# One pool of eight PSUM banks, and a biased order of work, in a kernel of two memory-attention and two gated layers

## The chip, the cores and the metric

The kernel runs on one core of one Trainium2 chip. The metric is the device time of one execution in microseconds (us), lower is better. Every time quoted is the median of the runs that are named with it; all runs here were in the same (fast) state, with a mean granted TensorE clock of 0.982 to 0.996 in their records. (The granted clock is the share of full speed at which the chip let TensorE run.) A ratio is the mean time of one kernel's runs over the mean of the other's runs of the same rounds, so it is not quite the ratio of the medians quoted beside it. Engines: PE is TensorE's matmul, PEld its weight load, DVE is VectorE, ACT is ScalarE, POOL is GpSimd.

## The reference, cut to what matters

Two layers of a memory-augmented attention A and a gated feed-forward B, applied twice with the same weights:

```python
x = x + A(layernorm(x));  x = x + B(layernorm(x))      # and the same two lines once more

def A(x):                            # 2048 rows, width 448, 16 heads of 256
    mem = mem0                       # 8 rows
    for s in range(64):              # 64 segments of 32 rows, one after the other
        h = concat([mem, x[32*s : 32*s+32]])             # 40 rows
        q, k, v = h @ Wq, h @ Wk, h @ Wv                 # per head
        p = softmax(mask(q @ k.T / 16))
        o = (p @ v) @ Wo
        mem = o[:8]                  # the next segment needs this
        outs.append(o[8:])

def B(x):                            # relu-gated: 448 -> 1792 -> 448
    return (relu(x @ Wg) * (x @ Wu)) @ Wd
```

The loop over segments is a recurrence: segment s+1 cannot form its keys before the eight memory rows of segment s are known. Layer 2 runs four segments behind layer 1, in the same matmuls, so there are 68 steps. Two steps are a pair; B is done once per pair.

## The kernel before

The kernel folds `Wq` with `Wk` into `M` and `Wv` with `Wo` into `N` once at the start. TensorE writes its results into eight PSUM banks, tensors of 128 x 512 float32; a copy of a result out of a bank by DVE or ACT is called an eviction below. Each step is made of small kinds of work, which the argument below calls by these names:

| kind | what TensorE does in it |
|---|---|
| `t_unit` | T = M times the step's 40 columns `hT`, 224 matmuls of 80 columns; DVE/ACT copy them to `TTm` and `TTs` |
| `s_mem`, `p_t_mem`, `u_mem`, `un_mem` | scores of the memory rows, transpose of P, U = P times `hK`, memory output = `UTm` times `N` (in 32-column tiles) |
| `m_t` | eight small selection matmuls that bring the new memory rows (kept as two bf16 tensors, `hi` and the rest `lo`), transposed, into `hT` (the T units of the next step need them) |
| `m_nat` | two matmuls that bring the same rows in natural layout into `hK` |
| `s_seg`, `seg_pt`, `u_seg` | the same for the 32 segment rows; U goes to `U` (inside the tensor named `big`) |
| `un` | attention output of a pair, 56 matmuls of 448 columns, `U` times `N` |
| `ln_b`, `b_layer`, `b_down`, `ln_a` | layer norm, gate/up, down, and the layer norm that makes the input of a later pair |

The program is first a list of operations with the keys that they read and write. (A tile in the code is a result that occupies a bank. The changes of tiling further below are another thing: TensorE's array, divided into parts for small matmuls.) A list scheduler then orders the operations with a model of the engines, and the engines run in that order. An operation's priority is the length of the longest path behind it:

```python
class _Order:
    POOLS = {"R": [0, 1, 2, 3, 5]}                     # five banks in a pool
    LAT = {"pe": 170.0, "act": 0.0, "dve": 0.0, ...}

    def graph(self):
        ...
        for o in reversed(self.ops):
            lat = ...
            o.prio = min(o.cost.values()) + max([q.prio + ... for q in o.succs], default=lat)

    def run(self):
        ...                     # for each engine: when could each candidate start?
            t0 = min(x[0] for x in lst)
            lim = max(f, t0) + (60.0 if e == "pe" else 40.0)
            t, o = max((x for x in lst if x[0] <= lim), key=lambda x: (x[1].prio, -x[0]))
        ...
        for tl in o.alloc:      # a tile takes the bank of its pool that is free first
            b = min(fr, key=lambda k: fr[k])
```

The other three banks have fixed roles: bank 4 (`bO`) for `un` and `b_down`, banks 6 and 7 (`bC`) for the memory's chain:

```python
self.bO, self.bC = bank[4], bank[6:8]

def m_t(self, t):
    b1, b0 = S.bC[1], S.bC[0]                                          # banks 7 and 6
    S.mm(... three groups into b1 ..., S.ps(7))
    S.mm(... the fourth group into b0[:, 448:464] ..., S.ps(6))
    S.cp(hT[..., 0:3, ...], b1[...], 48, S.ps(7), w, eng=("dve",))
    for half in range(2):
        S.cp(hT[64*half:..., 3, ...], b0[64:128, 448:464], 16, S.ps(6, half=(1,)), ..., eng=("act",))

def m_nat(self, t):
    b0 = S.bC[0]                                                       # bank 6 again
    S.mm(lambda: [MM(b0[:, 0:D], S.seln[:, :], x[:, :], ...) for i, x in enumerate((S.hi, S.lo))], ..., S.ps(6))
```

A last detail: the code that sets the semaphores lets two engines take turns on a bank even when both only read it.

```python
            if r[0] == "ps":
                for src, val in self.readers.get(r, {}).items():
                    if src != eng:
                        want(src, val)
```

Of the kernel before, what the change touches and what calls it, by code (L numbers as in the profile page):

```python
# [6 lines left out]
BF = dt.bfloat16  # L7
# [142 lines left out]

class _Tile:
# [12 lines left out]
class _Op:  # L164
    __slots__ = ("kind", "eng", "cost", "fn", "rd", "wr", "name", "mode", "preds", "succs", "prio", "np", "fin", "alloc", "tiles", "fixed", "lat")


class _Order:
# [5 lines left out]
    POOLS = {"R": [0, 1, 2, 3, 5]}  # L174

    def __init__(self, sched):
        self.sc = sched
        self.ops = []

    def add(self, kind, eng, cost, fn, rd, wr, name=None, mode=0, lat=None):  # L180
        o = _Op()
        o.kind, o.eng, o.cost, o.fn, o.rd, o.wr, o.name, o.mode = kind, eng, cost, fn, list(rd), list(wr), name, mode
        o.succs, o.np, o.alloc, o.fixed, o.lat = [], 0, [], None, lat
        self.ops.append(o)
        return o
# [9 lines left out]
    def graph(self):  # L195
# [26 lines left out]
        for o in reversed(self.ops):  # L222
            lat = self.LAT[o.eng[0]] if o.lat is None else o.lat
            o.prio = min(o.cost.values()) + max([q.prio + (0.0 if o.kind == q.kind == "pe" else lat + 60.0) for q in o.succs], default=lat)

# [143 lines left out]
class _Kernel:  # L369
# [16 lines left out]
    def alloc(self):  # L386
# [46 lines left out]
        self.bO, self.bC = bank[4], bank[6:8]  # L433
# [355 lines left out]
    def s_mem(self, t):  # L789
# [4 lines left out]
        b = S.bC[0]  # L794
        S.mm(lambda: [MM(b[:, l * KEYS:l * KEYS + KEYS], S.TTm[:, c, l, :], S.hT[:, pp, s, c, l, :], start=(c == 3), stop=(c == 2))
                      for l in range(l0, l1) for c in (3, 0, 1, 2)], 100.0 * nl,
             [("TTm",) + k for k in S.TKEYS] + [("hTx", pp, s)] + S.mkeys(pp, s, l0, l1), S.ps(6))
        st = S.stat
        src = b[:, l0 * KEYS:l1 * KEYS].rearrange("p (l x) -> p l x", l=nl)
# [3 lines left out]
        S.dve(lambda E: E.tensor_reduce(st[:, 32:32 + nl], src, AX.X, ALU.max), n, S.ps(6), [("sm", 0)])  # L803
        S.dve(lambda E: E.tensor_tensor(Em, src, bc(32), ALU.subtract), n, S.ps(6) + [("sm", 0)], [("Em",)])
# [51 lines left out]
    def p_t_mem(self, t):  # L856
        S = self
        pT = S.bC[1][:, :].bitcast(BF)
        S.mm(lambda: [MM(pT[:, 0:128], S.Pm[:, :], S.ident[:, :], is_transpose=True)], 60.0, [("Pm",), ("ident",)], S.ps(7))
        S.cp(lambda: S.PTm[:, :], lambda: pT[:, 0:128], 128, S.ps(7), [("PTm",)])  # L860
# [10 lines left out]
    def u_mem(self, t):  # L871
# [3 lines left out]
        S.mm(lambda: [m for c in range(4) for l in range(l0, l1) for m in S.u_mms(l, c, pp, s, S.bC[l][:, c * 128:], S.PTm, 8)], 350.0,  # L875
             [("PTm",)] + [("hKx", pp, s, l) for l in range(l0, l1)] + [("hKm", pp, s, l) for l in range(l0, l1)],
             S.ps(*[6 + l for l in range(l0, l1)]), mode=1)
        for l in range(l0, l1):
            S.cp(lambda l=l: S.UTm[:, 0:NO, l * 8:l * 8 + 8], lambda l=l: S.bC[l][:, 0:D].rearrange("p (o q) -> p o q", o=NO), D,
                 S.ps(6 + l), [("UTm", l)], eng=("act", "dve") if l1 - l0 == 1 else (("act", "dve")[l],))  # L880

    def un_mem(self, t):
        S = self
        b = S.bC[0]

        def mms():
            out = []
            for k in range(14):
                for j in range(4):
                    o = 14 * j + k  # L890
                    lhs = S.UTm[:, o:o + 2, :].rearrange("p a q -> p (a q)")
                    out.append(MM(b[32 * j:32 * j + 32, 0:D], lhs, S.N[:, o, :], start=(k == 0), stop=(k == 13)))
            return out

        S.mm(mms, 14 * S.pitch(D) + 100.0, [("UTm", 0), ("UTm", 1)] + (S.Nkeys if t == 0 else []), S.ps(6), mode=2)
        S.act(lambda E: E.activation(S.hi[:, :], b[:, 0:D], ACT.Copy), D, S.ps(6), [("hi",)])  # L896
        S.dve(lambda E: E.tensor_tensor(S.lo[:, :], b[:, 0:D], S.hi[:, :], ALU.subtract), D, S.ps(6) + [("hi",)], [("lo",)])  # L897

    def m_t(self, t):
# [5 lines left out]
        b1, b0 = S.bC[1], S.bC[0]  # L905
        sel = [("sel", j) for j in range(4)]
        S.mm(lambda: [MM(b1[:, c * 16:c * 16 + 16], x[:, c * 128:c * 128 + 128], S.selm[:, :], start=(i == 0), stop=(i == 1))
                      for c in range(3) for i, x in enumerate((S.hi, S.lo))], 150.0, [("hi",), ("lo",)] + sel, S.ps(7))
        S.mm(lambda: [MM(b0[:, 448:464], x[:, 320:448], S.selm[:, :], start=(i == 0), stop=(i == 1)) for i, x in enumerate((S.hi, S.lo))],
             50.0, [("hi",), ("lo",)] + sel, S.ps(6))  # L910
        w = [("hTm", pp, s, l) for l in range(l0, l1)]
        S.cp(lambda: S.hT[:, pp, s, 0:3, l0:l1, SEG:KEYS], lambda: b1[:, 0:48].rearrange("p (c l q) -> p c l q", c=3, l=2)[:, :, l0:l1, :],
             48, S.ps(7), w, eng=("dve",))
        v = b0[64:128, 448:464].rearrange("p (l q) -> p l q", l=2)[:, l0:l1, :]
        for half in range(2):
            S.cp(lambda half=half: S.hT[64 * half:64 * half + 64, pp, s, 3, l0:l1, SEG:KEYS], lambda: v, 16, S.ps(6, half=(1,)),
                 [("hTm3", pp, s, half)], eng=("act",))

    def m_nat(self, t):
# [3 lines left out]
        b0 = S.bC[0]  # L923
        S.mm(lambda: [MM(b0[:, 0:D], S.seln[:, :], x[:, :], start=(i == 0), stop=(i == 1)) for i, x in enumerate((S.hi, S.lo))],
             2 * S.pitch(D), [("hi",), ("lo",), ("sel",)] + [("sel", j) for j in range(4)], S.ps(6))
        for l in range(*S.layers(t)):
            if l == 1 and t == LAG:
                continue
# [153 lines left out]
```

## Time and profile before

1785.34 us, median of 3 runs (1779.55 to 1785.48). The profile's first part gives each engine's busy time, its share of the span and its instructions:

```profile
span 1780.3 us, 67770 instructions
PE 1700.7 (96%) x30612; PEld 1226.7 (69%) x30612; DVE 1073.2 (60%) x3058; ACT 720.6 (40%) x2031; POOL 91.0 (5%) x156
```

TensorE bounds the kernel, and the other engines have room. But a busy share of 96% does not say how much could be won, because a matmul's record is longer than the distance to the next one. So I worked from the starts of the matmuls in the trace. A matmul of 448 columns starts 189 ns after the one before, one of 128 columns 56 ns, one of 80 columns 36 ns, and one of 40 columns or fewer 25 ns. Where the tiles of the array change (whole array, 40 rows, 32 or 64 columns), the next start comes 95 ns later than that. Whatever remains of the distance between two starts is called waiting here. This splits the time from the first matmul to the last:

| before | us |
|---|---|
| all matmuls at their own pitch | 1578.5 |
| 721 changes of tiling, 95 ns each | 68.5 |
| waiting | 121.9 |
| of it steps 0 to 10 (with the weight loads) / steps 10 to 60 / the end | 37.8 / 65.0 / 19.1 |

Where the waiting is shows the view of who waited for whom. A line reads: engine, line and tile that waited, what it waited for, us in total, times, longest. These are TensorE's waits for copies of `hT`, for `xn` (the layer norm's output) and for the evictions of U (`big`):

```profile
PEld b L127 <- ACT hT L684: 30.1, 80, 0.6
PEld b L127 <- DVE xn L721: 27.4, 31, 5.6
PEld b L127 <- ACT big L684: 21.0, 47, 0.7
PE b L127 <- ACT hT L684: 14.9, 32, 0.5
PEld b L127 <- DVE big L685: 14.5, 28, 0.7
```

The longest regular one, in the timeline (start, duration, engine, line, operation, tiles, shape, count, idle before and releaser):

```profile
823.99 0.17 PE L127 MATMUL b<-selm,lo 128*128 128x16 bf16 x1
824.01 0.62 DVE L968 TENSOR_TENSOR XB<-b,XA 128x448 bf16<-128x448 f32 x1 [0.50 <-PE b L127]
824.20 0.38 ACT L684 ACTIVATE hT<-b 64x16 bf16<-64x16 f32 x2 [0.19 <-PE b L127]
824.55 0.20 DVE L685 CAST hT<-b 128x48 bf16<-128x48 f32 x1
...
824.64 0.36 PE L127 MATMUL b<-hi,seln 128*128 128x448 bf16 x1 [0.48 <-ACT hT L684]
```

The last selection matmul starts at 823.99. The natural-layout matmul (`hi,seln`) could follow at once, but it writes bank 6, which ACT still reads for `hT`, and it starts 0.65 us later.

### The profile page before, as it was taken

Reading aid. Unit: us, or ns where it says so; the run is one execution under the profiler, and the core shown is the slowest. Engines: PE = TensorE matmul, PEld = TensorE weight load, DVE = VectorE, ACT = ScalarE, POOL = GpSimd, SP = SyncE. Lnnn points to the kernel's source line nnn. Section 1 sums busy time; section 2 is a strip of 40 time slices with the busy share of each in tenths; the row PEclk is TensorE's granted clock in tenths of the full one; section 3 lists DMA queues with packets and bytes.
Section 4 is the critical chain, followed back from the end, with each engine's and each line's share of the span. In section 5 each row is a group of like instructions: output and inputs, shape, how many; then the busy total and the mean of one; then the engine's idle time right before and its main releaser. Section 6 shows DMA issues by size and latency. Waiting matters only on the chain.

```text
span 1780.3 us, 67770 instructions
## 1 busy us (share of the span) xinstructions
PE 1700.7 (96%) x30612; PEld 1226.7 (69%) x30612; DVE 1073.2 (60%) x3058; ACT 720.6 (40%) x2031; POOL 91.0 (5%) x156
## 2 busy tenths in 40 slices
PE   6899999999999999999999999999999999999997
PEld 2566766777677667767766776776677677667765
DVE  7647565565656556565655656565665656566554
ACT  5433433444443334444333444334344433434432
POOL 3000000000000000000000000000000000000000
PEclk9999999999999999999999999999999999999999
DMA  9700000000000000000000000000000000000000
GB/s 227 219 4 4 4 5 5 4 5 5 5 4 5 5 4 5 5 5 4 5 5 4 5 5 5 4 5 4 4 5 6 5 4 5 3 3 4 4 4 5
DMA packets 55760, 27.52 MB, mean 15 GB/s; under 512 B 44584, under 2 KB 54576, under 8 KB 55472
## 3 DMA queue, kind: packets, MB, share of 16 engines
q1 hardware_dynamic: 55120, 22.94, 5.3%
q8 instruction: 241, 3.95, 0.9%
q14 instruction: 47, 0.39, 0.1%
q10 hardware_dynamic: 352, 0.24, 0.1%
HBM read 10.33 MB, written 1.84 MB: 7 GB/s over the span
## 4 chain that ended last, share of the span: by engine, by line
PE 75%; DVE 6%; ACT 2%; issue 1%; DVEq 0%
PE b L127 75%; ACT big L684 1%; DVE big L685 1%; DVE stat L714 1%; DVE TTs L685 1%; DVE xn L721 1%; ACT hT L684 1%; DVE ys L1015 1%; DVE XA L1008 1%; DVE XB L968 0%; DVE Es L843 0%; DVE stat L842 0%; DVE TTm L685 0%; DVE hT L685 0%; DVE part L957 0%
## 5 line engine op out<-in xcount | busy, mean ns | idle before, releaser
L127 PEld LDWEIGHTS b<-hT,Mw 128*128 128x128 bf16 x15232 | 539.8, 100 | 25.3 <-DVE hT L685 11.2
L127 PE MATMUL b<-hT,Mw 128*128 128x80 bf16 (+1 forms) x15232 | 546.0, 200 | 5.0 <-DVE hT L685 4.6
L127 PE MATMUL b<-Nw,big 128*128 128x448 bf16 (+1 forms) x1936 | 394.9, 358 | 8.2 <-DVE big L685 5.6
L685 DVE CAST TTs<-b 128x320 bf16<-128x320 f32 (+5 forms) x574 | 261.3, 455 | 78.6 <-PE b L127 78.3
L127 PEld LDWEIGHTS b<-Nw,big 128*128 128x128 bf16 (+1 forms) x1936 | 163.7, 100 | 157.1 <-issue 21.5
L127 PE MATMUL b<-xBT,big 128*128 128x128 bf16 (+1 forms) x3808 | 219.6, 217 | 0.7 <-ACT xBT L684 0.7
L685 DVE CAST TTm<-b 128x80 bf16<-128x80 f32 (+5 forms) x580 | 134.7, 232 | 129.5 <-PE b L127 98.0
L127 PEld LDWEIGHTS b<-xBT,big 128*128 128x128 bf16 x3808 | 204.7, 98 | 2.4 <-ACT xBT L684 0.9
L127 PE MATMUL b<-Nw,UTm 128*32 128x448 bf16 x3752 | 192.0, 356 | 0.6 <-ACT UTm L684 0.6
L685 DVE CAST big<-b 128x512 bf16<-128x512 f32 (+1 forms) x190 | 121.3, 659 | 103.9 <-PE b L127 102.8
L684 ACT ACTIVATE big<-b 128x512 bf16<-128x512 f32 (+1 forms) x322 | 153.7, 525 | 48.2 <-PE b L127 45.0
L127 PEld LDWEIGHTS b<-Nw,UTm 128*32 128x32 bf16 x3752 | 95.2, 97 | 88.9 <-issue 18.7
L685 POOL COPY hK<-xn 32x448 bf16<-32x448 bf16 x136 | 75.6, 556 | 1521.6 <-DVE xn L721 1470.4
L684 ACT ACTIVATE TTs<-b 64x256 bf16<-64x256 f32 (+5 forms) x310 | 127.6, 412 | 29.6 <-PE b L127 22.4
L995 ACT ACTIVATE gT<-b 128x256 bf16<-128x256 f32 x226 | 86.4, 382 | 128.8 <-PE b L127 124.1
L684 ACT ACTIVATE TTm<-b 64x64 bf16<-64x64 f32 (+4 forms) x304 | 69.4, 228 | 159.4 <-PE b L127 152.5
L996 DVE TENSOR_TENSOR hB<-gT,b 128x256 bf16<-128x256 bf16 x226 | 93.6, 415 | 64.8 <-ACT gT L995 54.0
L896 ACT ACTIVATE hi<-b 128x448 bf16<-128x448 f32 x67 | 36.5, 544 | 193.7 <-PE b L127 193.5
L897 DVE TENSOR_TENSOR lo<-b,hi 128x448 bf16<-128x448 f32 x67 | 41.4, 619 | 121.2 <-ACT hi L896 121.2
L127 PE MATMUL b<-big,hB 128*128 128x448 bf16 (+1 forms) x476 | 107.3, 355 | 0.0
L684 ACT ACTIVATE hK<-b 8x448 bf16<-8x448 f32 x94 | 50.4, 536 | 122.5 <-PE b L127 121.0
L127 PE MATMUL b<-PTs,hK 40*128 40x512 bf16 (+1 forms) x640 | 86.4, 348 | 13.3 <-DVE XA L1008 7.1
(103 smaller groups left out, 1396.1 us busy)
## 6 DMA issues: line engine op xcount, KB each, us to landing
big<-in_A_Wo_dram SPq DMA_DIRECT2D x3, 896.0 KB, 5.8
out_dram<-ys SPq DMA_DIRECT2D x32, 56.0 KB, 1.9
big<-in_B_W_down_dram SPq DMA_DIRECT2D x1, 1568.0 KB, 6.8
XA<-in_A_x_dram SPq DMA_DIRECT2D x28, 56.0 KB, 2.0
big<-in_B_W_up_dram SPq DMA_DIRECT2D x1, 1344.0 KB, 8.1
big<-in_B_W_gate_dram SPq DMA_DIRECT2D x1, 1344.0 KB, 8.5
Nw<-in_A_Wo_dram SPq DMA_DIRECT2D x1, 896.0 KB, 6.4
XA<-in_A_x_dram ACTq DMA_DIRECT2D x4, 56.0 KB, 4.3
```

What stands on the lines that cost most here:

```text
L127: ins = E.matmul(out, lhsT=lhsT, rhs=rhs, **kw)
L684: return E.activation(out(), src(), ACT.Copy)
L685: return E.tensor_copy(out(), src())
L714: S.dve(lambda E: E.bn_stats(st[:, so:so + 6], x), D, rd, [(key, 0)])
L721: S.dve(lambda E, a=a, b=b, src=src: E.tensor_scalar(S.xn[:, i, a:b], src, st[:, so + 6:so + 7], st[:, so + 8:so + 9], op0=ALU.subtract, o ...
L896: S.act(lambda E: E.activation(S.hi[:, :], b[:, 0:D], ACT.Copy), D, S.ps(6), [("hi",)])
L897: S.dve(lambda E: E.tensor_tensor(S.lo[:, :], b[:, 0:D], S.hi[:, :], ALU.subtract), D, S.ps(6) + [("hi",)], [("lo",)])
L995: S.act(lambda E, k=k, R=R, n=n: E.activation(S.gT[:, k % 2, 0:n], R[0].b()[:, 0:n], ACT.Relu), n, R[0].res(), [("gT", k % 2)])
L996: S.dve(lambda E, k=k, R=R, n=n, fcs=fcs: E.tensor_tensor(S.hB[:, fcs[0]:fcs[-1] + 1, 0:w], S.gT[:, k % 2, 0:n].rearrange("p (a b) -> p a ...
L1008: S.dve(lambda E: E.tensor_tensor(S.XA[64:128, q % 4, :], S.bO[0:64, 0:D], S.XB[0:64, p % 2, :], ALU.add), D, S.ps(4, half=(0,)) + xb, [(" ...
L1015: S.dve(lambda E: E.tensor_tensor(S.ys[64:128, p % 2, :], S.bO[64:128, 0:D], S.XB[64:128, p % 2, :], ALU.add), D, S.ps(4, half=(1,)) + xb, ...
```

## The change

All eight banks form one pool that the scheduler deals from, and every kind of work gets a constant added to its priority. The constants were fitted offline with the scheduler's own engine model. The tiles `m_t` used in two banks become one tile. The diff, cut to its core:

```diff
+BIAS = {
+    "b_down": 10000.0, "b_layer": 59336.0, "ln_a": 27598.0, "ln_b": 5000.0, "m_nat": -1055.0, "m_t": 14051.0,
+    "p_t_mem": 31928.0, "s_mem": 11350.0, "s_seg": -1955.0, "seg_pt": 21197.0, "t_unit": 56079.0, "u_mem":
+    29620.0, "u_seg": 10869.0,
+}
-    POOLS = {"R": [0, 1, 2, 3, 5]}
+    POOLS = {"R": list(range(8))}
@@ graph
+        for o in self.ops:
+            o.prio += BIAS.get(o.cat, 0.0)
@@ alloc
-        self.bO, self.bC = bank[4], bank[6:8]
@@ s_mem, and likewise p_t_mem, u_mem, un_mem, m_nat, un, b_layer
-        b = S.bC[0]
+        C = S.tile("R", 1)
@@ m_t
-        S.mm(... c in range(3) into b1 ..., S.ps(7))
-        S.mm(... x[:, 320:448] into b0[:, 448:464] ..., S.ps(6))
+        S.mm(... all four groups into C.b()[:, c * 16:c * 16 + 16] ..., C.res() + mk)
-        S.cp(... b1 ..., 48, S.ps(7), w, eng=("dve",))
-        ... b0[64:128, 448:464] ..., 16, S.ps(6, half=(1,)), eng=("act",)
+        S.cp(... v()[:, 0:3], 48, C.res(), ..., eng=("dve",))
+        S.cp(... v()[64:128, 3], 16, C.res(half=(1,)), ..., eng=("act",))       # twice
@@ step
-            S.m_nat(t)
+            S.do("m_nat", t)          # sets the kind; so for every kind
```

(The other cuts are the same replacement of fixed banks by tiles, and extra keys on the matmuls so that a tile is not taken before its destination is free.)

More of the change, by code (lines that the diff above doesn't have):

```diff
@@ L164 @@
 class _Op:
-    __slots__ = ("kind", "eng", "cost", "fn", "rd", "wr", "name", "mode", "preds", "succs", "prio", "np", "fin", "alloc", "tiles", "fixed", "lat")
+    __slots__ = ("kind", "eng", "cost", "fn", "rd", "wr", "name", "mode", "preds", "succs", "prio", "np", "fin", "alloc", "tiles", "fixed", "lat", "cat")
 class _Order:
     ENGS = ("pe", "act", "dve", "pool", "sp")
-    POOLS = {"R": [0, 1, 2, 3, 5]}
+    POOLS = {"R": list(range(8))}
     def __init__(self, sched):
@@ L178, in __init__ @@
         self.ops = []
+        self.cat = ""
     def add(self, kind, eng, cost, fn, rd, wr, name=None, mode=0, lat=None):
@@ L182, in add @@
         o.kind, o.eng, o.cost, o.fn, o.rd, o.wr, o.name, o.mode = kind, eng, cost, fn, list(rd), list(wr), name, mode
-        o.succs, o.np, o.alloc, o.fixed, o.lat = [], 0, [], None, lat
+        o.succs, o.np, o.alloc, o.fixed, o.lat, o.cat = [], 0, [], None, lat, self.cat
         self.ops.append(o)
@@ L793, in s_mem @@
         nl = l1 - l0
-        b = S.bC[0]
-        S.mm(lambda: [MM(b[:, l * KEYS:l * KEYS + KEYS], S.TTm[:, c, l, :], S.hT[:, pp, s, c, l, :], start=(c == 3), stop=(c == 2))
+        C = S.tile("R", 1)
+        S.mm(lambda: [MM(C.b()[:, l * KEYS:l * KEYS + KEYS], S.TTm[:, c, l, :], S.hT[:, pp, s, c, l, :], start=(c == 3), stop=(c == 2))
                       for l in range(l0, l1) for c in (3, 0, 1, 2)], 100.0 * nl,
-             [("TTm",) + k for k in S.TKEYS] + [("hTx", pp, s)] + S.mkeys(pp, s, l0, l1), S.ps(6))
+             [("TTm",) + k for k in S.TKEYS] + [("hTx", pp, s)] + S.mkeys(pp, s, l0, l1), C.res())
         st = S.stat
-        src = b[:, l0 * KEYS:l1 * KEYS].rearrange("p (l x) -> p l x", l=nl)
+        src = lambda: C.b()[:, l0 * KEYS:l1 * KEYS].rearrange("p (l x) -> p l x", l=nl)
         bc = lambda a: st[:, a:a + nl].unsqueeze(2).to_broadcast([128, nl, KEYS])
@@ L802, in s_mem @@
         n = nl * KEYS
-        S.dve(lambda E: E.tensor_reduce(st[:, 32:32 + nl], src, AX.X, ALU.max), n, S.ps(6), [("sm", 0)])
-        S.dve(lambda E: E.tensor_tensor(Em, src, bc(32), ALU.subtract), n, S.ps(6) + [("sm", 0)], [("Em",)])
+        S.dve(lambda E: E.tensor_reduce(st[:, 32:32 + nl], src(), AX.X, ALU.max), n, C.res(), [("sm", 0)])
+        S.dve(lambda E: E.tensor_tensor(Em, src(), bc(32), ALU.subtract), n, C.res() + [("sm", 0)], [("Em",)])
         S.act(lambda E: E.activation(Fm, Em, ACT.Exp, scale=SCALE), n, [("Em",)], [("Fm",)])
@@ L857, in p_t_mem @@
         S = self
-        pT = S.bC[1][:, :].bitcast(BF)
-        S.mm(lambda: [MM(pT[:, 0:128], S.Pm[:, :], S.ident[:, :], is_transpose=True)], 60.0, [("Pm",), ("ident",)], S.ps(7))
-        S.cp(lambda: S.PTm[:, :], lambda: pT[:, 0:128], 128, S.ps(7), [("PTm",)])
+        C = S.tile("R", 1)
+        pT = lambda: C.b().bitcast(BF)
+        S.mm(lambda: [MM(pT()[:, 0:128], S.Pm[:, :], S.ident[:, :], is_transpose=True)], 60.0, [("Pm",), ("ident",)], C.res() + [("PTm",)])
+        S.cp(lambda: S.PTm[:, :], lambda: pT()[:, 0:128], 128, C.res(), [("PTm",)])
     def u_mms(self, l, c, pp, s, ps, PT, w):
@@ L874, in u_mem @@
         l0, l1 = S.layers(t)
-        S.mm(lambda: [m for c in range(4) for l in range(l0, l1) for m in S.u_mms(l, c, pp, s, S.bC[l][:, c * 128:], S.PTm, 8)], 350.0,
+        C = {l: S.tile("R", 1) for l in range(l0, l1)}
+        S.mm(lambda: [m for c in range(4) for l in range(l0, l1) for m in S.u_mms(l, c, pp, s, C[l].b()[:, c * 128:], S.PTm, 8)], 350.0,
              [("PTm",)] + [("hKx", pp, s, l) for l in range(l0, l1)] + [("hKm", pp, s, l) for l in range(l0, l1)],
-             S.ps(*[6 + l for l in range(l0, l1)]), mode=1)
+             [r for l in C for r in C[l].res()] + [("UTm", l) for l in C], mode=1)
         for l in range(l0, l1):
-            S.cp(lambda l=l: S.UTm[:, 0:NO, l * 8:l * 8 + 8], lambda l=l: S.bC[l][:, 0:D].rearrange("p (o q) -> p o q", o=NO), D,
-                 S.ps(6 + l), [("UTm", l)], eng=("act", "dve") if l1 - l0 == 1 else (("act", "dve")[l],))
+            S.cp(lambda l=l: S.UTm[:, 0:NO, l * 8:l * 8 + 8], lambda l=l: C[l].b()[:, 0:D].rearrange("p (o q) -> p o q", o=NO), D,
+                 C[l].res(), [("UTm", l)], eng=("act", "dve") if l1 - l0 == 1 else (("act", "dve")[l],))
     def un_mem(self, t):
         S = self
-        b = S.bC[0]
+        C = S.tile("R", 1)
         def mms():
@@ L891, in mms @@
                     lhs = S.UTm[:, o:o + 2, :].rearrange("p a q -> p (a q)")
-                    out.append(MM(b[32 * j:32 * j + 32, 0:D], lhs, S.N[:, o, :], start=(k == 0), stop=(k == 13)))
+                    out.append(MM(C.b()[32 * j:32 * j + 32, 0:D], lhs, S.N[:, o, :], start=(k == 0), stop=(k == 13)))
             return out
-        S.mm(mms, 14 * S.pitch(D) + 100.0, [("UTm", 0), ("UTm", 1)] + (S.Nkeys if t == 0 else []), S.ps(6), mode=2)
-        S.act(lambda E: E.activation(S.hi[:, :], b[:, 0:D], ACT.Copy), D, S.ps(6), [("hi",)])
-        S.dve(lambda E: E.tensor_tensor(S.lo[:, :], b[:, 0:D], S.hi[:, :], ALU.subtract), D, S.ps(6) + [("hi",)], [("lo",)])
+        S.mm(mms, 14 * S.pitch(D) + 100.0, [("UTm", 0), ("UTm", 1)] + (S.Nkeys if t == 0 else []), C.res() + [("hi",), ("lo",)], mode=2)
+        S.act(lambda E: E.activation(S.hi[:, :], C.b()[:, 0:D], ACT.Copy), D, C.res(), [("hi",)])
+        S.dve(lambda E: E.tensor_tensor(S.lo[:, :], C.b()[:, 0:D], S.hi[:, :], ALU.subtract), D, C.res() + [("hi",)], [("lo",)])
     def m_t(self, t):
@@ L904, in m_t @@
         l0 = max(l0, S.layers(t + 1)[0])
-        b1, b0 = S.bC[1], S.bC[0]
+        C = S.tile("R", 1)
         sel = [("sel", j) for j in range(4)]
-        S.mm(lambda: [MM(b1[:, c * 16:c * 16 + 16], x[:, c * 128:c * 128 + 128], S.selm[:, :], start=(i == 0), stop=(i == 1))
-                      for c in range(3) for i, x in enumerate((S.hi, S.lo))], 150.0, [("hi",), ("lo",)] + sel, S.ps(7))
-        S.mm(lambda: [MM(b0[:, 448:464], x[:, 320:448], S.selm[:, :], start=(i == 0), stop=(i == 1)) for i, x in enumerate((S.hi, S.lo))],
-             50.0, [("hi",), ("lo",)] + sel, S.ps(6))
-        w = [("hTm", pp, s, l) for l in range(l0, l1)]
-        S.cp(lambda: S.hT[:, pp, s, 0:3, l0:l1, SEG:KEYS], lambda: b1[:, 0:48].rearrange("p (c l q) -> p c l q", c=3, l=2)[:, :, l0:l1, :],
-             48, S.ps(7), w, eng=("dve",))
-        v = b0[64:128, 448:464].rearrange("p (l q) -> p l q", l=2)[:, l0:l1, :]
-        for half in range(2):
-            S.cp(lambda half=half: S.hT[64 * half:64 * half + 64, pp, s, 3, l0:l1, SEG:KEYS], lambda: v, 16, S.ps(6, half=(1,)),
-                 [("hTm3", pp, s, half)], eng=("act",))
+        mk = S.mkeys(pp, s, l0, l1)
+        S.mm(lambda: [MM(C.b()[:, c * 16:c * 16 + 16], x[:, w:w + 128], S.selm[:, :], start=(i == 0), stop=(i == 1))
+                      for c, w in ((0, 0), (1, 128), (2, 256), (3, 320)) for i, x in enumerate((S.hi, S.lo))], 200.0,
+             [("hi",), ("lo",)] + sel, C.res() + mk)
+        v = lambda: C.b()[:, 0:64].rearrange("p (c l q) -> p c l q", c=4, l=2)[:, :, l0:l1, :]
+        S.cp(lambda: S.hT[:, pp, s, 0:3, l0:l1, SEG:KEYS], lambda: v()[:, 0:3], 48, C.res(), mk[:-2], eng=("dve",))
+        S.cp(lambda: S.hT[0:64, pp, s, 3, l0:l1, SEG:KEYS], lambda: v()[64:128, 3], 16, C.res(half=(1,)), mk[-2:-1], eng=("act",))
+        S.cp(lambda: S.hT[64:128, pp, s, 3, l0:l1, SEG:KEYS], lambda: v()[64:128, 3], 16, C.res(half=(1,)), mk[-1:], eng=("act",))
     def m_nat(self, t):
@@ L922, in m_nat @@
         pp, s = (t // 2) % 2, t % 2
-        b0 = S.bC[0]
-        S.mm(lambda: [MM(b0[:, 0:D], S.seln[:, :], x[:, :], start=(i == 0), stop=(i == 1)) for i, x in enumerate((S.hi, S.lo))],
-             2 * S.pitch(D), [("hi",), ("lo",), ("sel",)] + [("sel", j) for j in range(4)], S.ps(6))
-        for l in range(*S.layers(t)):
-            if l == 1 and t == LAG:
-                continue
+        C = S.tile("R", 1)
+        ls = [l for l in range(*S.layers(t)) if not (l == 1 and t == LAG)]
+        S.mm(lambda: [MM(C.b()[:, 0:D], S.seln[:, :], x[:, :], start=(i == 0), stop=(i == 1)) for i, x in enumerate((S.hi, S.lo))],
+             2 * S.pitch(D), [("hi",), ("lo",), ("sel",)] + [("sel", j) for j in range(4)], C.res() + [("hKm", pp, s, l) for l in ls])
+        for l in ls:
             r = slice(64 * l + 32, 64 * l + 40)
-            S.cp(lambda r=r: S.hK[r, pp, s, :], lambda r=r: b0[r, 0:D], D, S.ps(6, half=(l,)), [("hKm", pp, s, l)])
+            S.cp(lambda r=r: S.hK[r, pp, s, :], lambda r=r: C.b()[r, 0:D], D, C.res(half=(l,)), [("hKm", pp, s, l)])
     def u_seg(self, t):
@@ L952, in rows, with halves @@
         return slice(0, 64) if p < LAG // 2 else slice(64, 128) if p >= NSEG // 2 else slice(0, 128)
-    def halves(self, dst, base, base_keys, r, keys):
+    def halves(self, O, dst, base, base_keys, r, keys):
         S = self
-        S.dve(lambda E: E.tensor_tensor(S.part[r, :], S.bO[0:64, 0:D], base, ALU.add), D, S.ps(4, half=(0,)) + base_keys, [("part",)])
-        S.dve(lambda E: E.tensor_tensor(dst, S.bO[64:128, 0:D], S.part[r, :], ALU.add), D, S.ps(4, half=(1,)) + [("part",)], keys)
+        S.dve(lambda E: E.tensor_tensor(S.part[r, :], O.b()[0:64, 0:D], base, ALU.add), D, O.res(half=(0,)) + base_keys, [("part",)])
+        S.dve(lambda E: E.tensor_tensor(dst, O.b()[64:128, 0:D], S.part[r, :], ALU.add), D, O.res(half=(1,)) + [("part",)], keys)
     def un(self, p):
@@ L962, in un @@
         r = S.rows(p)
+        O = S.tile("R", 1)
         uk = [[("U", s, l, c) for s in range(2) for l in range(2)] for c in range(4)]
@@ L965, in un @@
             for k in range(0, NO, 2):
-                S.mm(lambda k=k: [MM(S.bO[:, 0:D], S.U[:, o, :], S.N[:, o, :], start=(o == 0), stop=(o == NO - 1)) for o in (k, k + 1)],
-                     2 * S.pitch(D), uk[k // 16], S.ps(4))
-            S.dve(lambda E: E.tensor_tensor(S.XB[:, p % 2, :], S.bO[:, 0:D], S.XA[:, p % 4, :], ALU.add), D,
-                  S.ps(4) + [("XA", p % 4, 0), ("XA", p % 4, 1)], [("XB", p % 2)])
+                S.mm(lambda k=k: [MM(O.b()[:, 0:D], S.U[:, o, :], S.N[:, o, :], start=(o == 0), stop=(o == NO - 1)) for o in (k, k + 1)],
+                     2 * S.pitch(D), uk[k // 16], O.res())
+            S.dve(lambda E: E.tensor_tensor(S.XB[:, p % 2, :], O.b()[:, 0:D], S.XA[:, p % 4, :], ALU.add), D,
+                  O.res() + [("XA", p % 4, 0), ("XA", p % 4, 1)], [("XB", p % 2)])
         else:
             for k in range(0, NO, 4):
-                S.mm(lambda k=k: [MM(S.bO[64 * (o % 2):64 * (o % 2) + 64, 0:D], S.U[:, o, r], S.N[:, o, :], start=(o < 2), stop=(o >= NO - 2))
-                                  for o in range(k, k + 4)], 2 * S.pitch(D), uk[k // 16], S.ps(4), mode=6)
-            S.halves(S.XB[r, p % 2, :], S.XA[r, p % 4, :], [("XA", p % 4, r.start // 64)], r, [("XB", p % 2)])
+                S.mm(lambda k=k: [MM(O.b()[64 * (o % 2):64 * (o % 2) + 64, 0:D], S.U[:, o, r], S.N[:, o, :], start=(o < 2), stop=(o >= NO - 2))
+                                  for o in range(k, k + 4)], 2 * S.pitch(D), uk[k // 16], O.res(), mode=6)
+            S.halves(O, S.XB[r, p % 2, :], S.XA[r, p % 4, :], [("XA", p % 4, r.start // 64)], r, [("XB", p % 2)])
         S.load_x(p + 4)
@@ L998, in b_layer @@
                 R[1].b()[:, 0:n].rearrange("p (a b) -> p a b", b=w), ALU.mult), n, R[1].res() + [("gT", k % 2)], hk)
+        S.q.cat = "b_down"
         full = w == 128
+        O = S.tile("R", 1)
         for k in range(7):
-            S.mm(lambda k=k: [MM(S.bO[:, 0:D] if full else S.bO[64 * (fc % 2):64 * (fc % 2) + 64, 0:D], S.hB[:, fc, 0:w], S.Wd[:, fc, :],
+            S.mm(lambda k=k: [MM(O.b()[:, 0:D] if full else O.b()[64 * (fc % 2):64 * (fc % 2) + 64, 0:D], S.hB[:, fc, 0:w], S.Wd[:, fc, :],
                                  start=(fc < (1 if full else 2)), stop=(fc >= NFC - (1 if full else 2))) for fc in (2 * k, 2 * k + 1)],
-                 (2 if full else 1) * S.pitch(D), [("hB", k), ("Wd",)], S.ps(4), mode=0 if full else 6)
+                 (2 if full else 1) * S.pitch(D), [("hB", k), ("Wd",)], O.res(), mode=0 if full else 6)
         xb = [("XB", p % 2)]
@@ L1007, in b_layer @@
             if full:
-                S.dve(lambda E: E.tensor_tensor(S.XA[64:128, q % 4, :], S.bO[0:64, 0:D], S.XB[0:64, p % 2, :], ALU.add), D,
-                      S.ps(4, half=(0,)) + xb, [("XA", q % 4, 1)])
+                S.dve(lambda E: E.tensor_tensor(S.XA[64:128, q % 4, :], O.b()[0:64, 0:D], S.XB[0:64, p % 2, :], ALU.add), D,
+                      O.res(half=(0,)) + xb, [("XA", q % 4, 1)])
             else:
-                S.halves(S.XA[64:128, q % 4, :], S.XB[0:64, p % 2, :], xb, r, [("XA", q % 4, 1)])
+                S.halves(O, S.XA[64:128, q % 4, :], S.XB[0:64, p % 2, :], xb, r, [("XA", q % 4, 1)])
         if p >= LAG // 2:
@@ L1014, in b_layer, with do @@
             if full:
-                S.dve(lambda E: E.tensor_tensor(S.ys[64:128, p % 2, :], S.bO[64:128, 0:D], S.XB[64:128, p % 2, :], ALU.add), D,
-                      S.ps(4, half=(1,)) + xb, [("ys", p % 2)])
+                S.dve(lambda E: E.tensor_tensor(S.ys[64:128, p % 2, :], O.b()[64:128, 0:D], S.XB[64:128, p % 2, :], ALU.add), D,
+                      O.res(half=(1,)) + xb, [("ys", p % 2)])
             else:
-                S.halves(S.ys[64:128, p % 2, :], S.XB[64:128, p % 2, :], xb, r, [("ys", p % 2)])
+                S.halves(O, S.ys[64:128, p % 2, :], S.XB[64:128, p % 2, :], xb, r, [("ys", p % 2)])
             S.qdma(f"ys{p % 2}", lambda E: E.dma_start(S.o_d[64 * q:64 * q + 64, :], S.ys[64:128, p % 2, :]), (), [("ys", p % 2)])
+    def do(self, name, *args):
+        self.q.cat = name
+        getattr(self, name)(*args)
+        self.q.cat = ""
     def step(self, t):
@@ L1026, in step @@
         if t > 0:
-            S.m_nat(t)
+            S.do("m_nat", t)
         for k in S.UNITS:
-            S.t_unit(t, *k)
+            S.do("t_unit", t, *k)
         if not last:
-            S.s_mem(t)
-            S.p_t_mem(t)
-            S.u_mem(t)
-            S.un_mem(t)
-            S.m_t(t)
+            S.do("s_mem", t)
+            S.do("p_t_mem", t)
+            S.do("u_mem", t)
+            S.do("un_mem", t)
+            S.do("m_t", t)
             if t + 1 == LAG:
                 S.start_mem(1)
-        S.s_seg(t)
-        S.seg_pt(t)
-        S.u_seg(t)
+        S.do("s_seg", t)
+        S.do("seg_pt", t)
+        S.do("u_seg", t)
         if s == 1:
             if p == 0:
-                S.ln_a(1)
-            S.un(p)
-            S.ln_b(p)
-            S.b_layer(p)
+                S.do("ln_a", 1)
+            S.do("un", p)
+            S.do("ln_b", p)
+            S.do("b_layer", p)
             if p + 2 < NP:
-                S.ln_a(p + 2)
+                S.do("ln_a", p + 2)
 _INS = ['A_x', 'A_mem0', 'A_Wq', 'A_Wk', 'A_Wv', 'A_Wo', 'A_seg_len', 'B_x', 'B_W_gate', 'B_W_up', 'B_W_down']
```

## The prediction

> **What bounds it now.** TensorE. In the table of busy times PE has 96% of 1780 us, DVE 60%, ACT 40%; the chain of waits is 75% PE. I used the starts of consecutive matmuls in the timeline: one of 448 columns starts 189 ns after the last, of 80 columns 36 ns, of 128 columns 56 ns. Every matmul at its own pitch makes about 1578 us. Where the shape of the weight tile changes (whole array, 40-row, 32-column tiles) the next start comes 95 ns later than the pitch. The Trainium skill, "TensorEngine Tiling (Array Packing)", Key Properties, says that changing the tiling mode drains the TensorE; this trace agrees, at 95 ns. Some 720 changes make 68 us. The other 122 us are PE waiting: 25 us in the first 100 us (partly weight loads), 73 us in the steady part (200 to 1650 us), 24 us in the rest.
>
> **The steady 73 us**, by what starts late (28 pairs of segments, 51.8 us each):
> - 17 us: the memory's natural-layout matmul waits 0.62 us after the selection matmuls, until ScalarE has copied out of the same fixed bank 6.
> - 14 us: the layer-norm transpose waits for xn, whose input came late from the GLU layer.
> - 11 + 9 + 4 us: the U matmuls, and what follows them, wait for a pool bank or an eviction (5 banks, evictions of 0.6 to 0.7 us).
> - 6 us: the T units wait for the memory columns of hT.
> - 4.5 us: segment scores wait for the last TTs/TTm copies.
>
> **What the change does.** No work goes away. Fixed banks 4, 6 and 7 join the pool, so bank 6 no longer orders memory scores, memory output, selection and natural layout, nor bank 4 attention output and GLU down. The skill, "Perfetto Trace Analysis", Matmul Optimizations, asks for all 8 banks; here the fixed-bank wait of 17 us is what that can win. The bias moves gate/up and T units ahead and leaves attention output (10.6 us a pair) as filler. It should bring the layer-norm input earlier.
>
> Added: the hT copies now share a bank, so ACT (0.38 us) and DVE (0.20 us) take turns: about 0.2 us more on the memory recurrence per step, at most 13 us if nothing filled it. From the timeline's durations I estimate 17 to 18 us for one pass of the recurrence against 26 us per step, so filler can hide it.
>
> **On the critical path.** All PE waiting is. The bound is 1578 + 68 + some 15 us of loading, near 1660 us. I expect steady waits to fall from 73 to about 25 us, start and tail by 5 us together, tiling changes by 0 to 5 us. The bias was fitted to a model, so part of its gain won't show: net about 50 us.
>
> **Predicted: 1735 us, 8 in 10 between 1705 and 1766.** Faster by over 2%: 0.70; within 2%: 0.28; slower by over 2%: 0.02.
>
> **What would show it.** Right: the natural-layout matmul no longer begins 0.6 us late; PE's waits for DVE xn, ACT hT and big shrink; the pair's period falls from 51.8 to about 50.3 us; DVE and ACT busy sums stay within 2%. Wrong: new PE waits of similar size elsewhere (T units waiting for serialized hT copies), or more tiling changes than 720 because U matmuls are scattered.
>
> **What would make it wrong.** If the stalls come from a lack of ready work rather than of banks, freeing banks gains only part, and the time stays near 1760. If the search also found far fewer tiling changes, it goes below 1705.

## The result, and the profile after

1713.4 us, median of 4 runs (1712.55 to 1714.38), against 1783.68 us of before (4 runs): ratio 0.9609, 95% interval 0.9589 to 0.9629. That is 70 us, faster than the predicted 1735 and inside its range. All runs were correct.

The same first part, after:

```profile
span 1712.3 us, 67944 instructions
PE 1671.6 (98%) x30612; PEld 1228.4 (72%) x30612; DVE 1106.3 (65%) x3157; ACT 670.6 (39%) x1932; POOL 90.7 (5%) x156
```

PE has exactly as many matmuls. Some evictions went from ACT to DVE (99 instructions), because the scheduler chooses the engine of a copy too. PE's busy sum fell by 29 us all the same: about 6 us of it are matmuls at a slower clock (below); I take the rest to be short waits that lay hidden inside the overlapping records, but it was not tested.

The window of 200 to 1600 us shows the same from the side of throughput. The columns are the window, its length, and then busy time and count for PE, PEld, DVE, ACT and POOL, then clock, DMA share and GB/s. Before:

```profile
200.00:1600.00 1400.00, 1359.96 (x24376) 992.27 (x24376) 841.69 (x2347) 569.04 (x1600) 60.08 (x108) 1.00 0.02 5
```

After:

```profile
200.00:1600.00 1400.00, 1394.27 (x25590) 1041.73 (x25583) 907.12 (x2544) 553.13 (x1593) 62.25 (x112) 1.00 0.02 5
```

In the same 1400 us TensorE ran 25590 matmuls instead of 24376, and was idle for 5.7 us (1400 - 1394.27) instead of 40.0.

The waits after, for the same releasers:

```profile
PEld b L127 <- DVE xn L731: 25.9, 34, 5.8
PEld b L127 <- ACT big L694: 17.3, 47, 0.6
PEld b L127 <- DVE big L695: 5.9, 16, 0.4
PEld b L127 <- ACT hT L694: 0.9, 2, 0.6
PE b L127 <- ACT hT L694: 0.6, 2, 0.4
```

The wait for ACT's `hT` copies, 45 us in the two rows of before, is 1.5 us. The timeline at the corresponding place shows how:

```profile
825.39 0.17 PE L127 MATMUL b<-selm,lo 128*128 128x16 bf16 x1
825.39 0.88 PEld L127 LDWEIGHTS b<-Nw,big 128*128 128x128 bf16 x6
825.42 1.29 PE L127 MATMUL b<-Nw,big 128*128 128x448 bf16 x6
825.60 0.21 DVE L695 CAST hT<-b 128x48 bf16<-128x48 f32 x1 [1.06 <-PE b L127]
825.90 0.38 ACT L694 ACTIVATE hT<-b 64x16 bf16<-64x16 f32 x2 [2.37 <-DVE hT L695]
...
826.55 0.23 PE L127 MATMUL b<-hT,Mw 128*128 128x80 bf16 x2
```

Six matmuls of the attention output (`Nw,big`) stand between the selection matmuls and the T units, and outlast both copies: the second ACT copy ends at 826.28, the T units start at 826.55. `m_nat` is not even there: it comes about 13 us later. Note that the copies do take turns now, DVE first and then ACT, and nobody on TensorE notices.

The split by starts of matmuls, for both:

| | before | after |
|---|---|---|
| matmuls at their own pitch | 1578.5 | 1578.5 |
| changes of tiling | 721 = 68.5 us | 645 = 61.3 us |
| waiting | 121.9 | 61.6 |
| of it steps 0 to 10 / 10 to 60 / the end | 37.8 / 65.0 / 19.1 | 35.3 / 13.7 / 12.5 |
| period of a pair (steps 10 to 60) | 51.75 | 49.48 |

So 60.3 us of waiting and 7.2 us of tiling changes went, 67.5 us of the 68.0 us between the two profiled spans. 51.3 us of the waiting came from the steady part. The row of matmuls is the same by construction: both kernels have the same matmuls, each charged its pitch.

Not all of this waiting is waiting. Between 200 and 1650 us of before, four stretches of 3.4 us have a granted clock of 0.5, and in them matmuls of 448 columns start 373 ns apart instead of 189. This is one of them, first as a window (columns as above) and then in the timeline:

```profile
592.40:595.40 3.00, 3.00 (x9) 1.18 (x8) 1.70 (x4) 2.01 (x5) 0.90 (x2) 0.50 0.00 0
592.18 3.94 PE L127 MATMUL b<-Nw,big 128*128 128x448 bf16 x11 [0.37 <-DVE big L685]
```

By the starts of the matmuls each such stretch costs about 1.5 us, all four about 6 us; after has none between 200 and 1650 us. So about 6 of the 60.3 us are a faster clock and not less waiting. Why the clock dips came with the one order and not with the other was not tested.

### The profile page after: what moved, and what is told of

The parts are those of the page before. It is cut to its first block, busy times and chain, and to the rows that moved or that the text cites. A ratio compares the mean times of both kernels' runs of the same rounds, so it can differ in the third digit from the quotient of the medians.

```text
span 1712.3 us, 67944 instructions
## 1 busy us (share of the span) xinstructions
PE 1671.6 (98%) x30612; PEld 1228.4 (72%) x30612; DVE 1106.3 (65%) x3157; ACT 670.6 (39%) x1932; POOL 90.7 (5%) x156
## 5 line engine op out<-in xcount | busy, mean ns | idle before, releaser
L127 PE MATMUL b<-hT,Mw 128*128 128x80 bf16 (+1 forms) x15232 | 539.6, 200 | 3.4 <-issue 2.3
L127 PEld LDWEIGHTS b<-hT,Mw 128*128 128x128 bf16 x15232 | 534.0, 100 | 11.5 <-issue 3.2
L127 PE MATMUL b<-Nw,big 128*128 128x448 bf16 (+1 forms) x1936 | 389.8, 353 | 0.4 <-DVE big L695 0.2
L695 DVE CAST TTs<-b 128x320 bf16<-128x320 f32 (+5 forms) x565 | 257.5, 456 | 65.7 <-PE b L127 65.3
L127 PE MATMUL b<-xBT,big 128*128 128x128 bf16 (+1 forms) x3808 | 208.0, 217 | 1.2 <-ACT xBT L694 0.7
L127 PEld LDWEIGHTS b<-Nw,UTm 128*32 128x32 bf16 x3752 | 100.9, 98 | 86.6 <-ACT UTm L694 13.0
L694 ACT ACTIVATE big<-b 128x512 bf16<-128x512 f32 (+1 forms) x291 | 144.8, 553 | 43.0 <-PE b L127 42.1
L694 ACT ACTIVATE TTs<-b 64x256 bf16<-64x256 f32 (+4 forms) x319 | 130.8, 410 | 62.5 <-PE b L127 60.0
L695 DVE CAST big<-b 128x512 bf16<-128x512 f32 (+1 forms) x221 | 128.0, 607 | 21.2 <-PE b L127 19.6
L694 ACT ACTIVATE hT<-b 64x16 bf16<-64x16 f32 (+2 forms) x139 | 25.6, 185 | 124.5 <-DVE hT L695 114.0
```

The lines of the kernel that those rows point to most:

```text
L127: ins = E.matmul(out, lhsT=lhsT, rhs=rhs, **kw)
L694: return E.activation(out(), src(), ACT.Copy)
L695: return E.tensor_copy(out(), src())
```

## The experiments

The change has two parts, and three theories could explain the gain. A: the freed banks do it. B: the order (the bias) does it. C: each needs the other. The first four runs were made to tell these apart. All times are medians of 4 runs unless said otherwise, and each ratio is to the kernel before in the same rounds.

### 1. The pool alone

```diff
-BIAS = {"b_down": 10000.0, "b_layer": 59336.0, ...}
+BIAS = {}
```

> The kernel after, with an empty table of biases: eight banks in one pool, no bias. Theory A (the freed banks are the cause): at most 1735 us, and most of the 60 us of PE waiting are gone. Theory B (the bias, that is the order of the work, is the cause): at least 1765 us, waits still near 110 us in all. Theory C (each needs the other): both single parts give clearly less than 70 us in sum.

Measured: 1765.88 us (1765.36 to 1766.52), ratio 0.990 (0.9886 to 0.9915). The waiting is 109.9 us, 677 changes of tiling. Theory A falls: the eight pooled banks (with the merged selection and the extra keys of after) are worth 18 us of 70 with the unbiased priorities. The natural-layout matmul no longer waits, but the T units that follow it now start late by 25.3 us in all in the window of 200 to 1650 us, where before had 6.2 us there.

### 2. The bias alone

The kernel before, with its fixed banks, plus only the table and the line that adds it:

```diff
+BIAS = {...the same table...}
+        for o in self.ops:
+            o.prio += BIAS.get(o.cat, 0.0)
```

> The kernel before, fixed banks 4, 6 and 7 kept, with the same table of biases. Theory A: 1765 us or more. Theory B: at most 1735 us. Theory C: between, about 1750 us, because the table was found for eight pooled banks.

Measured: 1745.86 us (1744.84 to 1749.46), ratio 0.9792 (0.9775 to 0.9808). Waiting 95.3 us, 625 changes of tiling. The two parts alone give 18 and 38 us, together 70. That looks like theory C. But the table was fitted to a different arrangement of banks, so run 5 asks the fair question.

### 3. The fourth selection matmul moved, banks otherwise fixed

The code of after, without biases, and with every tile back in its old fixed bank. Against before, this changes (and the four groups are one operation, with the extra keys that after puts on its matmuls):

```diff
-        S.mm(... b0[:, 448:464] ..., S.ps(6))         # fourth group in bank 6, where m_nat writes
+        ... all four groups in bank 7 ...
```

> The kernel after without biases and with the old fixed banks, so that the only change against before is that the fourth selection matmul goes to bank 7 with the other three, and bank 6 no longer holds back the natural-layout matmul. If that bank is what costs 17 us in before, the wait of 0.62 us goes and the time falls by about 15 us, to 1768. If PE only has nothing else ready at that point, the natural-layout matmul starts at once but T units wait for the hT copies instead, and the time stays within 5 us of 1784.

Measured: 1800.22 us (1798.01 to 1801.42), ratio 1.0089 (1.0071 to 1.0106): slower by 16 us, which neither branch of the expectation had. In this order the 17 us at the natural-layout matmul were not the bank's to give back. The timeline of this run at the same place:

```profile
835.77 0.62 DVE L996 TENSOR_TENSOR XB<-b,XA 128x448 bf16<-128x448 f32 x1 [0.50 <-PE b L127]
835.77 0.35 PE L127 MATMUL b<-hi,seln 128*128 128x448 bf16 x1
...
835.96 0.38 ACT L712 ACTIVATE hT<-b 64x16 bf16<-64x16 f32 x2 [0.19 <-PE b L127]
835.96 0.35 PE L127 MATMUL b<-lo,seln 128*128 128x448 bf16 x1
...
836.44 0.21 DVE L713 CAST hT<-b 128x48 bf16<-128x48 f32 x1
...
836.79 0.20 PE L127 MATMUL b<-hT,Mw 128*128 128x80 bf16 x1 [0.48 <-DVE hT L713]
```

The natural-layout matmul now starts right behind the selection matmuls, at 835.77. Then TensorE waits all the same, for the `hT` copies, because the T units are next and nothing else stands in the order. In the window of 200 to 1650 us, the late starts of `m_nat` and of the T units behind it were 17.4 + 6.2 us before; here the T units alone have 24.9 us. So the loss of 16 us does not come from here. It sits in other places of a reshuffled order (the attention output waits 22.5 us behind U matmuls, before 8.8), and in the clock: between 200 and 1650 us this run has eight stretches at a granted clock of 0.5, which cost about 12 us, where the four of before cost 6. (The mean clock of its four runs is 0.983 to 0.985, of before's in the same rounds 0.989 to 0.991.) Since the merged operation and the extra keys came in with the bank, the run does not separate them.

### 4. The same order, banks dealt anew

After the scheduler has run, the order on every engine is kept as it is, and the banks are handed out again from all eight, longest free first:

```diff
         self.q.run()
+        self.q.redeal(8)      # first and last use of each tile in the order give its life; order untouched
         self.q.emit()
```

> Exactly the order of part_old on every engine, but the banks are dealt out afterwards from all eight, the one longest free first. Only the waits for banks on the chip can change, not the order. Theory A: at least 15 us faster than part_old. Theory B: within 5 us of part_old.

Measured: 1800.54 us (1794.67 to 1801.4), ratio 1.0087 against 1.0089. Waiting 140.1 us against 140.7. In this order the chip never missed a bank. What fixed banks cost, I conclude, lies in what the scheduler may put next to what; the order of before itself was not re-dealt.

### 5. Fixed banks, with a bias of their own

The kernel before with fixed banks, five pooled, and a table searched for this arrangement:

```diff
+BIAS = {"b_down": 20919, "b_layer": 37068, "ln_a": 36186, "ln_b": -41416, "m_nat": 56071, "m_t": 64805,
+        "p_t_mem": 113427, "s_mem": 69415, "s_seg": -121849, "seg_pt": 21592, "t_unit": 75025, "u_mem": 35483,
+        "u_seg": 25908, "un_mem": -795, "un": -711}
```

> The kernel before with its fixed banks 4, 6 and 7 and its five-bank pool, and a table of biases searched anew for exactly this arrangement (random changes to the table, kept where the scheduler's own length of the program fell). Theory C1 (pooled banks are needed for a good order): 1735 us or more. Theory B1 (any arrangement of the banks can be ordered well; the gain of pooling is only that it moves the unbiased order, and that the shipped table fits it): within 10 us of the kernel after, 1705 to 1725 us, PE waits near 65 us.

Measured: 1715.89 us (1714.49 to 1719.41), ratio 0.9621 (0.9602 to 0.9641). The kernel after has 0.9609 (0.9589 to 0.9629). The intervals overlap widely. Waiting 63.7 us, 632 changes of tiling, period 49.62 us. So theory B holds in this form: an order that fits the banks at hand gives the gain, and pooling them is not needed for it. What run 2 lacked was not banks, but a table made for its banks.

### 6. The order of after, from six and from seven banks

This is the counter-test to run 4, with the same `redeal`, now on the order of after, which never holds more than six tiles at once:

```diff
         self.q.run()
+        self.q.redeal(6)      # and 7
         self.q.emit()
```

> Exactly the order of the kernel after on every engine, but the banks are dealt from six instead of eight; two banks stay empty. If the chip needs eight banks so that TensorE does not wait for evictions, this is slower than after by 15 us or more. If banks matter only while the order is made, it is within 5 us of after, near 1713 us.

> The order of the kernel after, banks dealt from seven. Six gave 1744 us. If the dense cluster of U matmuls fills the banks, seven lies between, near 1725 us; if seven suffice, near 1713 us; a dealing rule that is bad in itself would show here too, but after_split used the same rule with eight banks and lost nothing.

Measured with six: 1744.5 us (1741.7 to 1747.1), ratio 0.9779 (0.9758 to 0.98). With seven: 1718.63 us (1715.78 to 1722.49), ratio 0.9645 (0.9624 to 0.9667), against 0.963 (0.9608 to 0.9651) of the unchanged kernel after on that chip, which is no clear difference. The dealing rule itself is harmless with eight banks (run 7). With six, the waits for U's evictions have grown:

```profile
PEld b L127 <- ACT big L733: 44.9, 77, 1.0
PE b L127 <- ACT big L733: 19.6, 44, 0.6
PEld b L127 <- DVE big L734: 16.5, 46, 1.5
```

They are 81.0 us, against 23.2 us in the corresponding lines of after (17.3 + 5.9; its `PE` rows for ACT `big` do not appear). The second branch of my expectation failed here: banks do count on the chip, for an order that was made while eight were free. I take the reason to be that it packs the U matmuls, two banks each, densely; that was not tested, nor whether six banks dealt by a better rule than longest-free-first would lose less. Seven fell between the two branches expected. This order is bound to more banks than it holds tiles at once.

### 7. The two hT copies in separate banks, orders kept

The prediction named one added cost: `m_t` in one bank makes DVE and ACT take turns. Here the fourth group gets a bank of its own when the program is written out, with the order of every engine unchanged:

```diff
-        MM(C.b()[:, c * 16:c * 16 + 16], ...)
+        MM((C if c < 3 else D2).b()[:, c * 16:c * 16 + 16], ...)     # and ACT reads D2
```

> Exactly the order of the kernel after, but the fourth group of selection matmuls goes to a bank of its own, so that ScalarE's two hT copies need not take turns with DVE's. The prediction said up to 13 us of cost if nothing filled it, and that filler hides it: then this is within 3 us of after. If the shared bank costs, it is 5 to 13 us faster.

> Exactly the order of part_old (1800 us), with the same split of the hT copies over two banks. If part_old lost its 16 us because the hT copies take turns on one bank in front of the T units (25 us of late starts there), this is 10 to 20 us faster than part_old, near 1785 us. If the loss is in the order that the scheduler made, it stays within 5 us of 1800.

Measured: on the order of after 1713.95 us (1711.12 to 1716.64), ratio 0.961, the same as after. On the order of run 3, 1796.71 us (1796.45 to 1797.47), ratio 1.0072 (1.0056 to 1.0089) against 1.0089 (1.0071 to 1.0106), 3.5 us by the medians, from rounds on two occasions, with overlapping intervals. Taking turns costs nothing where filler stands behind `m_t`, and little even where none does. So most of the 16 us that run 3 lost are not in the shared bank, but in its order and the slower clock that came with it.

### 8. Only the two largest biases

```diff
-BIAS = {"b_down": 10000.0, "b_layer": 59336.0, ...}
+BIAS = {"b_layer": 59336.0, "t_unit": 56079.0}
```

> The kernel after with only the two largest biases left: T units and gate/up (56079 and 59336), all others zero. The prediction held that moving these two ahead and leaving the attention output as filler is what the bias does. If so, this is near after, 1725 us or less. If the small terms matter as much, because every term is relative to the others, it is near the unbiased pool, 1760 us or more.

Measured: 1761.87 us (1759.24 to 1765.66), ratio 0.9888 (0.9866 to 0.9911); the pool with no bias at all had 0.990. Lifting T units and gate/up over everything else is worth next to nothing. So these two terms do not carry the gain by themselves. Which of the smaller terms do, and whether these two are needed beside them, was not tried.

### 9. A longer search

The kernel after with a table searched for longer, over the 13 kinds and also `un` and `un_mem`, and two numbers of the scheduler searched with it:

```diff
-            lim = max(f, t0) + (60.0 if e == "pe" else 40.0)
+            lim = max(f, t0) + (18.0 if e == "pe" else 40.0)
-            key=lambda x: (x[1].prio, -x[0])
+            key=lambda x: (x[1].prio + (493.0 if e == "pe" and x[1].mode == mode else 0.0), -x[0])
+BIAS = {'b_down': 9337, 'b_layer': 70486, 'ln_a': 2976, 'ln_b': 6180, 'm_nat': -1966, 'm_t': 22682,
+        'p_t_mem': 11563, 's_mem': 90415, 's_seg': -4694, 'seg_pt': 104884, 't_unit': 103894,
+        'u_mem': 99605, 'u_seg': 9817, 'un': -1988, 'un_mem': 1322}
```

> A try for a version faster than both: the kernel after with a table searched for longer, over 15 kinds, and with two more numbers of the scheduler searched, how far it looks past the earliest ready matmul (18 instead of 60 ns) and a small bonus for staying in the tiling mode. The scheduler's own length fell by 9 us against after. If its model carries over, 1700 to 1708 us; if the gain is fitted to the model alone, within 3 us of after.

> The kernel after, unchanged, as control for the run named best on the same chip: 1713 us within 2 us.

Measured: 1705.37 us (5 runs, 1702.05 to 1708.94), ratio 0.9571 (0.9549 to 0.9594). The unchanged kernel after on the same chip: 1716.36 us (1712.58 to 1719.04), ratio 0.963 (0.9608 to 0.9651), which is 3 us over its first median and just outside the 2 us that were expected. So this is 11 us faster than after and 78 us faster than before, by the medians. The waiting is 57.6 us, and the changes of tiling fell from 645 to 595, which is 4.8 us at 95 ns each. In the steady part TensorE waits 9.5 us in 50 steps. There is little waiting left to order away there; what an order could still remove is some of the 595 changes of tiling, 56.5 us. The table and the two numbers were changed together, so their shares are not known.

All runs side by side, split as above:

The last column is the part of the waiting that is slow clock, from the starts of the matmuls in the stretches at a granted clock of 0.5 between 200 and 1650 us.

| run | us | changes of tiling | waiting, us | period of a pair, us | half clock, us |
|---|---|---|---|---|---|
| before | 1783.68 | 721 | 121.9 | 51.75 | 6 |
| 3: fixed banks, selection moved | 1800.22 | 724 | 140.7 | 52.11 | 12 |
| 1: pool only | 1765.88 | 677 | 109.9 | 50.86 | 1 |
| 8: pool, two biases | 1761.87 | 687 | 101.9 | 50.80 | 0 |
| 2: bias only, made for the pool | 1745.86 | 625 | 95.3 | 50.01 | 0 |
| 5: fixed banks, own bias | 1715.89 | 632 | 63.7 | 49.62 | 0 |
| after | 1713.4 | 645 | 61.6 | 49.48 | 0 |
| 9: longer search | 1705.37 | 595 | 57.6 | 49.15 | 0 |

## Why the prediction was right or wrong

- **What bounds the kernel, and how much could be won: right.** The split into 1578 us of matmuls, 68 us of tiling changes and 122 us of waiting served, except that it has no term for the clock: about 6 of the steady 73 us were matmuls at a granted clock of 0.5. 67.5 of the 68.0 us between the profiled spans are in the other two terms.
- **The size: short by 20 us.** The prediction said "net about 50 us", and 70 us came. The terms that were too small: "steady waits to fall from 73 to about 25 us" in a window of equal length, where they fell to 18.0 us, about 6 us of it by the clock; and tiling changes "by 0 to 5 us", where they gave 7.2 us. Start and tail "by 5 us together" was right: outside the window of 200 to 1650 us the waiting fell by 5 us. These three terms made 53 to 58 us, and then the prediction took a discount because "the bias was fitted to a model, so part of its gain won't show". Nothing of it failed to show: the scheduler's own length fell by 62 us from before to after, and the chip's time by 70, of which about 6 are clock; in run 9 it fell by 9 us and the chip's time by 11 us.
- **"The fixed-bank wait of 17 us is what that can win": wrong as a mechanism.** Counted by banks, the advice was already met: before uses all eight, three of them in fixed roles. Run 3 takes this wait away and is 16 us slower. TensorE waits for the `hT` copies one instruction later, because nothing else was next in the order. That pooling alone won 18 us agrees with the predicted number by luck: in run 1 the T units behind the natural-layout matmul start late by 25.3 us instead of 6.2 us, so the 17 us were not won at this place, and about 5 of the 18 us are slow clock that went (1 us instead of 6).
- **"What would make it wrong", a lack of ready work rather than of banks: this was the truth where it was tested**, for the unbiased order of run 3 (run 4: eight banks for the same order change nothing). For the order of before itself it was not run. Freeing banks alone did end near 1760 us (run 1, 1766 us). The whole change did not, because the bias supplied the ready work at the right places.
- **"The bias moves gate/up and T units ahead and leaves attention output as filler": half right.** The filler is seen in the timeline of after, between selection matmuls and T units. But lifting only these two kinds gives 1762 us (run 8), so that is not what the table's gain comes from.
- **The added turn-taking of ACT and DVE, hidden by filler: right.** Undoing it changes nothing (run 7: 1713.95 us).
- **The signs.** The late natural-layout matmul is gone, and waits for ACT `hT` and for `big` shrank, as said. The waits for `xn` hardly did: 27.4 us in the `PEld` row before, 25.9 after. The period fell to 49.48 us, further than the predicted 50.3. DVE and ACT sums did not stay within 2%: DVE rose by 3.1% (1073.2 to 1106.3) and ACT fell by 6.9% (720.6 to 670.6), because the scheduler reassigned copies; that cost nothing, as neither engine binds.

What stays open: which terms of the table matter; whether fixed banks would keep up under the longer search of run 9, which was run for pooled banks only; and why the order of run 3 is so much worse than that of before, from which it differs in one bank of one small matmul, in the merging of that matmul with three others and in the extra keys. The scheduler did not foresee it: its own lengths for the two are 1762.7 and 1765.1 us, 2 us apart, where the chip shows 16. About 6 us of the rest are the clock's; what brings the clock down, and the remainder, stay open. The scheduler is greedy, and a small edit can move much else in it; that is an argument, not a finding.

## What to carry to other kernels

A wait on a buffer is only worth its length if something useful stands behind it: remove the buffer's conflict and see whether the next instruction waits for the same copies. Compare the granted clock of the two traces before a longer distance between matmuls is called waiting. Where a program is ordered by a model, judge a change of resources only after the order has been searched again for it. Here fixed and pooled banks ended 2.5 us apart by the medians once each had its own table, while a table carried over to the other arrangement lost 30 us.

## What the Trainium skill lacked or had wrong

- "Perfetto Trace Analysis", Matmul Optimizations, asks for all 8 PSUM banks to be used. It lacks that the order of the work can matter more than how the banks are shared out. Before already used all eight; with an order made for it, fixed banks came to 1715.89 us against 1713.4 us with a pool; eight banks dealt to an order made for fixed ones changed nothing (1800.54 against 1800.22 us), while six instead of eight cost the order of after some 30 us (1744.5 against 1713.95 us of the run with eight re-dealt).
- "TensorEngine Tiling (Array Packing)", Key Properties, says that changing the tiling mode drains the TensorE, with no figure. Here each change put the next start 95 ns beyond the pitch, and 595 to 724 of them made 57 to 69 us.
- "TensorE: Matmul & The Clock Gate", Back-to-back issue gap, gives about 81 ns per matmul of 128 columns in a real stream of weight loads and matmuls, and calls its formula of N/2.4 + 2.5 ns the isolated gap. In this kernel's streams, with a weight load for each matmul, the distance is 56 ns at 128 columns, 36 ns at 80 and 189 ns at 448, as that formula has it.
